# The first q and k of an attention kernel loaded by halves of the heads, deeper gates on the loads that follow, and a new order

## The chip, the cores and the metric

The kernel runs on one core of one Trainium2 chip. The metric is the device time of one execution in microseconds (us); lower is better. Engines are named as in the profile: PE is the matrix engine (PEld its weight loads), DVE the vector engine, ACT the scalar engine, POOL GpSimd, SP the engine that issues stores and DMA transposes here.

## The reference, cut to what matters

```python
# q, k, v: (4, 8, 768, 64) fp32; w_theta, w_ch: (512, 512); w_tok_r, w_tok_i: (768, 768)
scores = q @ k^T / 8                               # per batch and head
keep   = (key < 8) | (0 <= query - key < 96)       # 8 global keys, a local window of 96
scores = where(keep, scores - slope[h] * dist, -1e9)
x      = softmax(scores) @ v                       # then heads side by side: (4, 768, 512)
theta  = x @ w_theta
y      = w_tok_r @ (x * cos(theta)) + w_tok_i @ (x * sin(theta))   # mixes tokens
u      = x + y
out    = u + relu(u @ w_ch)                        # (4, 768, 512) fp32
```

## The kernel before

**Tiling.** A batch of 768 tokens is cut into three thirds of 256 tokens, each of two tiles of 128. Batch `b` and third `g` give names such as `t100`: most names in the order end in batch, third, then head pair, tile or half. Because the window is 96 wide, a tile of queries needs its own tile of keys and the one before it, plus the 8 global keys; a copy of the keys with the global ones put in place of its first eight tokens (`kp`, `kg`; `vpa`, `vpb` for the values) serves as "the one before".

**Stages.** For each third: q and k come in with the tokens on the partitions, PE transposes them (`t`, L371), DVE or ACT takes them out of PSUM (`q`, `k`, L380), PE makes the scores (`s`, L451), ACT the exponentials (`x`, L474), PE the values (`v`, L504), DVE divides by the sums (`n`, L515 and L517). In batch 0 the bias is put into PSUM first by a matmul of a scaled identity `sid` with a distance table `dtab` (`bi`, L442); in batches 1 to 3 the exponential is multiplied by a table `etab` on DVE (`m`, L482). After a batch: `xt` turns x (on PE for batches 0 and 1, as a DMA transpose on SP's queue for 2 and 3, L537), `th` is the theta matmul (L549), `cos` and `sin` run on ACT, `z` is the product on DVE, `mx` the token mixing on PE (L592), `u` the sum on DVE, `ut` turns it (on PE for batch 0, by DMA for the others, L624), `ch` is the last matmul (L636), `o` its end on DVE, `st` the store. `tw` and `twc` turn the token weights once.

**Loads.** The first third of batch 0 comes in fp32 by four DMAs of SP's and ACT's queues (`hw00` and `hw01` for q, `hw10` and `hw11` for k) and is cast on DVE (`cast`, L288). Everything else comes as bf16 by 82 DMAs that POOL issues (`load1` to `load82`): 1 to 4 are the second third's q and k, 5 to 8 values, 9 to 12 the last third's q and k, 13 and 14 values, 15 `w_theta`, 16 to 19 the first token weights, 20 to 49 batch 1, `w_ch` (`load28`) and the other token weights (up to `load44`), 50 to 82 batches 2 and 3. From `load20` on each has a gate in front, a 1x1 POOL copy that reads what the load `DEPTH` = 5 places before it has brought (L230). Besides, DMAs of POOL use eight semaphores in turn, so a load waits in any case until the one eight places before it has landed.

**Order.** All engines work in order, and the order is one long list, `ORDER`, written out in the kernel. `name/ENGINE` picks the engine of an operation that could run on two; `name+N` puts N filler matmuls on zeros in front of it on PE (L145, L147). PSUM has four buffers `pa` (biases, scores, theta) and four `pb` (the rest). Eight matmuls on zeros (L341) open the PE's list.

The lines that the change touches most are `first` (L274), `load_qk` and the calls of `batch` (L310 to L334), `trans_qk` (L361) and the `sid` operations (L209).

Of the kernel before, what the change touches and what calls it, by code (L numbers as in the profile page):

```python
# [9 lines left out]
FP = mybir.dt.float32  # L10
# [27 lines left out]
ones6 hw00 hw10 zero rel ones3 tiny hw01 halfpi hw11 warm0 ones5 ones1 ones4 ones2 load1 ones0 ident sid0 far0  # L38
sid2 far1 load2 dtab0 dtab1 dtab2 load3 dtab3 sid4 sid5 etab7 sid1 sid6 sid7 load4 sid3 etab6 bi0000
cast00/DVE bi0001 bi0010 etab3 load5 t0000 cast10/DVE bi0011 q000/DVE etab1 t0010+5 load6 k000/DVE etab2 kg000  # L40
kp000/DVE load7 etab0 cast01/DVE etab5 t0001+27 load8 cast11/DVE etab4 q001/DVE t0011+12 load9 k001/DVE kg001
s000+3 kp001/DVE load10 s001 x0000 x0001 load11 bi0020+3 t0100 x0010 x0011 bi0021 bi0030 load12 q010/DVE t0110
bi0031 s003 k010/DVE load13 s002 x0030 kg010 kp010/DVE x0031 load14 vpa00/DVE x0020 vpb00/DVE x0021 bi0100+6
load15 v003 v000 v001 load16 bi0101 n000 s010 vpa01/DVE load17 bi0110 x0100 bi0111 vpb01/DVE s011 load18 x0101
n003 bi0120 v002 x0110 load19 n001 bi0121 s012 x0111 n002 bi0130 x0120 v010 bi0131 n010 s013 x0121 v011 x0130
v012 n011 t0200 x0131 n012 t0210 q020/ACT bi0200 k020/DVE xt00 bi0201 xc00/ACT bi0210 kp020/DVE bi0211 kg020
v013 vpa02/DVE s020 n013 s021 x0200 vpb02/DVE xt01+6 x0201 bi0220 gate20 x0210 xc01/DVE bi0221+1 load20 v020
x0211 s022 n020 tw00 gate21 x0220 v021 load21 twc00/DVE bi0230 x0221 bi0231 n021 s023 gate22 th000 x0230
load22 x0231 v022 tw10 ts0 gate23 n022 tw11 load23 v023 twc10/DVE th001 n023 gate24 twc11/ACT load24 tw01 xt02
cos000 twc01/DVE gate25 th011 sin000 load25 xc02/DVE cos001 z000 gate26 th010 load26 sin001 th020 z001 cos010  # L50
gate27 load27 sin010 th021 cos011 z010 gate28 t1000 sin011 load28 tw21 cos020 q100/DVE mx000 gate29 sin020
twc21/DVE load29 t1010 cos021 z011 gate30 mx010 sin021 k100/DVE load30 tx1 vpa10/DVE mx001 gate31 kg100 load31
vpb10/DVE z020 mx011 gate32 kp100/DVE load32 z021 tw20 s100 twc20/DVE s101 gate33 mx002 x1000 load33 x1001
x1010 mx012 u00 x1011 gate34 load34 s102 m101 s103 tw30 u01 x1020 gate35 mx020 x1021 m100 load35 x1030 m102
x1031 mx022 gate36 twc30/DVE load36 m103 mx021 gate37 load37 ut00 u02 ut01 uc00/ACT v102 gate38 t1110 uc01/DVE
load38 tw31 k110/DVE ch01 twc31/ACT gate39 kp110/DVE load39 t1100 kg110 o01 v101 v103 q110/DVE gate40 v100
st01 tw41 load40 ch00 n100 twc41/ACT n101 gate41 ut02 load41 tw40 vpa11/DVE uc02/ACT mx030 o00 twc40/ACT
gate42 vpb11/DVE load42 st00 mx032 n102 n103 mx031 gate43 load43 s110 gate44 u03 s111 load44 x1100 t1200 ch02
x1110 gate45 q120/DVE load45 x1101 ut03 x1111 t1210 m110 gate46 uc03/ACT s112 load46 m111 s113 k120/ACT mx040
o02 gate47 x1120 load47 mx041 kp120/DVE st02 x1121 kg120 gate48 x1130 tw51 m112 load48 v110 twc51/ACT tw50  # L60
n110 v111 mx042 gate49 x1131 n111 load49 twc50/ACT vpa12/DVE s120 u04 s121 gate50 x1200 mx050 load50 m113
x1210 vpb12/DVE ut04 x1201 gate51 ch03 uc04/DVE load51 x1211 m120 s122 o03 gate52 s123 x1220 mx051 load52 m121
x1230 st03 v113 x1221 gate53 xt10 n113 load53 x1231 mx052 m122 ts1 gate54 v120 load54 u05 v112 v121 v122 n112
xc10/ACT ut05 gate55 ch04 n120 load55 uc05/DVE th100 vpa20/DVE gate56 m123 load56 ch05 cos100 vpb20/DVE n121
gate57 sin100 v123 load57 xt11 n122 th101 n123 xc11/ACT gate58 load58 o04 xt12 cos101 o05 th110 st04 gate59
sin101 xc12/DVE load59 st05 th111 cos110 z100 gate60 sin110 th121 z101 load60 cos111 z110 th120 sin111 gate61
vpa21/DVE load61 z111 t2100 cos120 t2010 gate62 vpb21/DVE sin120 load62 t2000 q210/DVE cos121 mx110 z120
gate63 sin121 q200/DVE load63 mx111 k200/ACT z121 gate64 t2110 tx2 load64 kg200 mx112 kp200/DVE k210/DVE
gate65 s200 u11 load65 s201 mx100 x2000 kp210/DVE x2001 ut11 kg210 gate66 x2010 mx101 m200 load66 x2011 s202
m201 gate67 s203 t2200 vpa22/DVE load67 x2020 x2021 t2210 vpb22/DVE x2030 q220/DVE v200 gate68 mx102 x2031  # L70
load68 n200 k220/ACT s210 m203 gate69 s211 m202 load69 x2100 mx120 kp220/DVE x2101 u10 gate70 mx122 x2110
load70 m210 x2111 ut10 s212 kg220 gate71 v202 m211 v201 x2120 load71 ch11 n202 x2121 n201 gate72 v203 s213
load72 n203 mx140 x2130 m212 xt20 gate73 x2131 v210 load73 vpa30/DVE s220 n210 v211 x2200 mx121 gate74 n211
x2201 load74 vpb30/DVE s221 m220 s222 gate75 x2210 ch10 load75 u12 x2211 m213 v220 x2220 ut12 mx130 gate76
x2221 m221 load76 s223 n220 v221 gate77 x2230 m222 mx141 load77 x2231 n221 v222 ts2 gate78 v212 m223 mx131
load78 n212 v223 gate79 n222 v213 load79 mx132 n223 n213 gate80 th200 xt22 load80 o11 mx142 vpa31/DVE cos200
gate81 xt21 u13 load81 sin200 ch12 vpb31/DVE u14 gate82 th201 ut13 load82 o12 mx150 o10 cos201 ut14 z200
sin201 mx151 z201 st12 mx152 st11 th221 st10 u15 t3110 ut15 t3010 k310/DVE t3000 k300/DVE t3100 kp310/ACT
th211 q300/DVE q310/ACT kp300/DVE th210 kg300 kg310 vpa32/DVE th220 cos210 vpb32/DVE sin210 t3210 cos211 t3200
z210 ch13 k320/ACT q320/DVE mx200 sin211 kp320/DVE cos220 o13 ch14 sin220 z211 st13 cos221 mx210 z220 sin221  # L80
o14 mx201 tx3 z221 st14 s300 kg320 s301 mx202 x3000 x3010 mx212 x3001 u20 x3011 m300 s302 ut20 s303 m301 ch15
x3020 x3021 x3030 mx211 o15 x3031 s310 m303 st15 s311 u21 x3100 mx220 x3101 m302 ut21 v300 x3110 mx222 m310
x3111 n300 mx221 m311 v301 u22 v303 v302 v310 n302 ch20 ut22 n301 mx230 o20 n303 ch21 st20 n310 xt30 s312 o21
s313 x3120 mx232 x3121 st21 v311 x3130 mx231 n311 x3131 m312 s320 s321 u23 x3200 mx240 x3201 m313 ut23 v312
x3210 ch22 n312 x3211 m320 s322 s323 o22 x3220 mx241 x3230 m321 st22 v313 x3221 mx250 n313 x3231 m322 ts3 v321
xt31 v320 m323 mx252 n320 v322 v323 n321 ch23 n323 th300 n322 o23 xt32 mx242 cos300 sin300 th301 u24 st23 z300
th310 ut24 cos301 sin301 mx251 cos310 z301 th311 sin310 u25 mx300 z310 cos311 ut25 sin311 th320 z311 th321
cos320 sin320 mx301 cos321 z320 ch24 sin321 z321 mx310 o24 mx302 st24 mx312 u30 mx311 ut30 ch25 u31 mx320 ut31
o25 mx322 st25 mx321 ch30 u32 mx330 ut32 o30 mx331 st30 ch31 mx332 o31 mx340 st31 u33 mx341 ut33 mx342 ch32
u34 mx350 ut34 o32 mx352 st32 mx351 ch33 u35 ut35 o33 ch34 uc35/ACT st33 ch35 o34 ch351 o35 st34 o351 st35  # L90
st351
# [4 lines left out]
def kernel(  # L96
# [13 lines left out]
    nc = tc.nc  # L110
# [51 lines left out]
    DEPTH = 5  # L162
# [46 lines left out]
    for h in range(H):  # L209
        add(f"sid{h}", {"DVE": 0.14},  # L210
            lambda h=h: nc.vector.tensor_scalar(sid[:, h], rel[:, 0], 0.0, -slopes[h] / scale,
                                                op0=ALU.is_equal, op1=ALU.mult),
            reads=["rel"], writes=[("sid", h)], prio=-5)
# [60 lines left out]
    def first(i, t):  # L274
        key, st = ("qk", 0, 0), ("stage", i, t)
        eng = ("SP", "ACT")[i]

        def fn():
            a = new(st, "e", [T, H, D], FP)
            (nc.sync, nc.scalar)[i].dma_start(out=a, in_=(q, k)[i][0, :, t * T:(t + 1) * T, :].rearrange("h p d -> p h d"))  # L280

        add(f"hw{i}{t}", {eng: 0.5}, fn, writes=[st], alloc={st: "e"}, prio=-300 + t,
            lat=(0.9, (0.98, 0.7, 1.75, 0.88)[2 * t + i], 1.45), after=["hw00"] if i + t else [])

        def cast():
            if key not in tiles:
                new(key, "qk", [T, 2, 2, DM], BF)
            vector[o.took](out=tiles[key][:, i, t].rearrange("p (h d) -> p h d", d=D), in_=tiles[st])  # L288

        o = add(f"cast{i}{t}", {"DVE": 0.34, "ACT": 0.49}, cast, reads=[st], writes=[key, key + (i, t)],  # L290
                alloc={key: "qk"} if (i, t) == (0, 0) else None, after=["cast00"] if (i, t) != (0, 0) else [])
# [446 lines left out]
```

The softmax here doesn't subtract the row's maximum and nothing guards it: scores larger than these inputs give would overflow.

## Time and profile before

| | us |
|---|---|
| median of 13 runs | 173.7 |
| lowest and highest of them | 172.57, 175.48 |
| the profiled execution's own time | 173.7 |
| its span, first to last instruction | 171.9 |
| PE busy | 162.7 (95%) |
| DVE busy | 133.9 (78%) |
| ACT busy | 105.9 (62%) |
| POOL busy | 84.1 (49%), all of it before 104 us |

The profiled execution agrees with the median, so its 1.8 us outside the span can be taken as fixed. A busy PE is not the same as a PE at its peak: the ends of matmuls are modelled, and fillers count as busy. So the rows by stage are read together with the starts of the matmuls in the timeline. The granted TensorE clock is 1.00 in every row from the start to the last slice.

### The profile page before, as it was taken

The page shows a single profiled execution, that of the slowest core. Times are in us where ns is not written, and L with a number is a line of the kernel's source. Part 1 is how long each engine was busy: PE and PEld are TensorE (multiplying, and loading weights), DVE is VectorE, ACT ScalarE, POOL GpSimd, SP SyncE. Part 2 cuts the span into 40 slices and gives each one's busy share as a digit, 9 for nine tenths or more (in the row PEclk, how much of TensorE's full clock was granted, in tenths as well). Part 3 has the DMA queues.
Part 4 walks back from the last instruction along what each step waited for, and adds up shares of the span by engine and source line. Part 5 has one row for each costly group of instructions (what it writes and reads, how often), then busy time and mean ns, then how long its engine had stood idle before and what let it go on. Part 6 is the DMA issues. An engine that isn't in the chain of part 4 may idle for free.

```text
span 171.9 us, 4153 instructions
## 1 busy us (share of the span) xinstructions
PE 162.7 (95%) x1598; PEld 92.9 (54%) x1623; DVE 133.9 (78%) x315; ACT 105.9 (62%) x187; POOL 84.1 (49%) x150
## 2 busy tenths in 40 slices
PE   7998999999999899999999999899999999999991
PEld 2664776555666456664555545544555644444440
DVE  7948886798898699999998997695987976634442
ACT  3954988996446887899867622799517847300010
POOL 8997249769897699698888870000000000000000
PEclk9999999999999999999999999999999999999999
DMA  5999999999999999999999999912345365134334
GB/s 123 187 154 155 188 175 117 157 175 150 151 163 191 183 113 157 98 197 121 126 138 139 136 139 164 273 65 87 96 107 138 103 81 131 57 91 127 93 92 183
DMA packets 96868, 23.73 MB, mean 138 GB/s; under 512 B 91088, under 2 KB 93904, under 8 KB 96848
## 3 DMA queue, kind: packets, MB, share of 16 engines
q0 software_dynamic: 73504, 12.33, 97.4%
q1 hardware_dynamic: 21264, 10.62, 25.4%
q10 hardware_dynamic: 2080, 0.52, 1.7%
q8 instruction: 12, 0.20, 0.5%
q14 instruction: 8, 0.07, 0.1%
HBM read 25.69 MB, written 6.29 MB: 186 GB/s over the span
## 4 chain that ended last, share of the span: by engine, by line
DMA 41%; PE 38%; POOL 11%; issue 6%; DVE 1%; DVEq 0%; POOLq 0%
PE pb L592 20%; DMA qk<-in_q_dram 15%; PE pb L636 8%; DMA qk<-in_k_dram 6%; DMA w_theta_bf<-in_moe_w_theta_dram 5%; PE pa L549 5%; DMA xT<-x 4%; POOL qk L243 4%; DMA w_nat<-in_moe_w_tok_i_dram 4%; POOL scrap L230 4%; DMA w_ch_bf<-in_moe_w_ch_dram 3%; DMA vn<-in_v_dram 3%; POOL vn L257 3%; PE pa L504 2%; PE pa L451 2%
## 5 line engine op out<-in xcount | busy, mean ns | idle before, releaser
L592 PE MATMUL pb<-zri,w_tokT 128*128 128x512 bf16 x273 | 67.3, 380 | 1.1 <-issue 0.5
L474 ACT ACTIVATE e<-pa 128x512 bf16<-128x512 f32 (+1 forms) x96 | 46.6, 568 | 20.6 <-PE pa L451 19.9
L592 PEld LDWEIGHTS <-w_tokT 128*128 128x128 bf16 x288 | 26.2, 98 | 28.2
L604 DVE TENSOR_TENSOR u<-x,pb 128x512 bf16<-128x512 bf16 x24 | 16.4, 682 | 11.4 <-PE pb L592 11.2
L636 PE MATMUL pb<-w_ch_bf,uT 128*128 128x512 bf16 (+1 forms) x96 | 24.0, 371 | 0.2
L549 PE MATMUL pa<-w_theta_bf,xT 128*128 128x512 bf16 x93 | 22.5, 380 | 0.5 <-DMA xT<-x 0.4
L482 DVE TENSOR_TENSOR e<-e,etab 128x1024 bf16<-128x1024 bf16 (+1 forms) x36 | 22.4, 637 | 0.7 <-ACT e L474 0.5
L558 ACT ACTIVATE cs<-pa,halfpi 128x512 bf16<-128x512 f32 x24 | 16.6, 692 | 9.8 <-PE pa L549 9.6
L257 POOL DMA_DIRECT2D vn<-in_v_dram x24 | 21.5, 899 | 1.6 <-issue 1.4
L243 POOL DMA_DIRECT2D qk<-in_q_dram x22 | 19.5, 884 | 1.6 <-issue 0.8
L570 DVE TENSOR_TENSOR zri<-x,cs 128x1024 bf16<-128x1024 bf16 x24 | 16.1, 683 | 5.3 <-ACT cs L560 5.3
L243 POOL DMA_DIRECT2D qk<-in_k_dram x22 | 19.4, 881 | 0.6 <-issue 0.6
L642 DVE SCALAR_TENSOR_TENSOR o<-pb,u 128x512 f32<-128x512 f32 (+1 forms) x25 | 16.2, 662 | 3.8 <-PE pb L636 3.7
L504 PEld LDWEIGHTS <-e 128*128 128x128 bf16 x352 | 14.4, 98 | 5.2 <-DVE e L482 0.3
L517 DVE TENSOR_TENSOR x<-pa,rec 128x256 bf16<-128x256 f32 x36 | 15.3, 424 | 1.2
L451 PE MATMUL pa<-qT,kk 64*128 64x128 bf16 x352 | 15.4, 218 | 0.4 <-DVE x L517 0.2
L451 PEld LDWEIGHTS <-kk 64*128 64x128 bf16 x352 | 10.0, 94 | 10.1 <-issue 8.0
L620 ACT COPY uT<-pb 128x512 bf16<-128x512 bf16 x4 | 2.4, 595 | 20.9 <-PE pb L616 20.9
L549 PEld LDWEIGHTS <-xT 128*128 128x128 bf16 x96 | 8.9, 98 | 10.5 <-DMA xT<-x 0.5
L560 ACT ACTIVATE cs<-pa 128x512 bf16<-128x512 f32 x24 | 14.4, 601 | 0.0
L371 PE MATMUL pb<-ident,qk 128*128 128x128 bf16 x192 | 13.7, 220 | 0.4 <-DVE qk L288 0.3
L636 PEld LDWEIGHTS <-uT 128*128 128x128 bf16 x100 | 9.0, 98 | 8.4 <-ACT uT L620 0.3
(69 smaller groups left out, 207.3 us busy)
## 6 DMA issues: line engine op xcount, KB each, us to landing
out_dram<-o SPq DMA_DIRECT2D x23, 256.0 KB, 2.4
vn<-in_v_dram POOLq DMA_DIRECT2D x24, 128.0 KB, 5.5
qk<-in_q_dram POOLq DMA_DIRECT2D x22, 128.0 KB, 5.6
qk<-in_k_dram POOLq DMA_DIRECT2D x22, 128.0 KB, 5.5
w_nat<-in_moe_w_tok_r_dram POOLq DMA_DIRECT2D x6, 192.0 KB, 5.9
w_nat<-in_moe_w_tok_i_dram POOLq DMA_DIRECT2D x6, 192.0 KB, 6.4
e<-in_k_dram ACTq DMA_DIRECT2D x2, 256.0 KB, 5.7
e<-in_q_dram SPq DMA_DIRECT2D x2, 256.0 KB, 5.0
```

The lines of the kernel that those rows point to most:

```text
L243: nc.gpsimd.dma_start(out=tiles[key][:, i, t].rearrange("p (h d) -> p h d", d=D), in_=(q, k)[i][b, :, r0:r0 + T, :].rearrange("h p d -> p ...
L257: nc.gpsimd.dma_start(out=v_bufs[i][:, t, :, 0:D], in_=v[b, :, r0:r0 + T, :].rearrange("h p d -> p h d"))
L451: nc.tensor.matmul(p_[hh][:, s], lhsT=tiles["kk", b, kg][R, kt, p, r, :], rhs=tiles["qT", b, g][R, qt, p, :], start=not biased, stop=not b ...
L474: nc.scalar.activation(tiles[ek][:, hh, 0:n], tiles[pb[hh]][:, 0:n], AF.Exp, scale=scale)
L482: nc.vector.tensor_mul(e_[:, :, 0:n], e_[:, :, 0:n], etab[:, 2 * p:2 * p + 2, s0:s0 + n])
L504: nc.tensor.matmul(o, lhsT=l_, rhs=r_, start=(i == 0), stop=(i == len(mms) - 1))
L549: nc.tensor.matmul(p_, lhsT=tiles["xT", b, g][:, p, t, :], rhs=w_theta_bf[:, p, :], start=(p == 0), stop=(p == NP - 1))
L558: nc.scalar.activation(tiles[ck][:, 0], tiles[ps], AF.Sin, bias=halfpi)
L592: nc.tensor.matmul(p_, lhsT=w_tokT[wi][:, 2 * g + t, tt * T:(tt + 1) * T], rhs=tiles["z", b, g][:, t, wi, :], start=(n == 1 and t == 0 and ...
L604: nc.vector.tensor_add(u.rearrange("n (p c) -> n p c", p=NP), tiles["x", b, tt // 2][:, :, tt % 2, :], tiles[ps].rearrange("n (p c) -> n p ...
L636: nc.tensor.matmul(p_, lhsT=tiles["uT", b, tt][:, p, :], rhs=w_ch_bf[:, p, i * w:(i + 1) * w], start=(p == 0), stop=(p == NP - 1))
L642: nc.vector.scalar_tensor_tensor(o_[:, c], in0=tiles["ch", b, tt, i], scalar=0.0, in1=tiles[uk][:, c], op0=ALU.max, op1=ALU.add)
```

## The change

The four first loads no longer split by tokens but by heads: `hw00` brings q of heads 0 to 3 for all 256 tokens, `hw01` that of heads 4 to 7, and likewise for k. Partition p gets the tokens 2p and 2p+1, which lie side by side in memory, so a run is 512 bytes where it was 256, and there are 512 runs per load where there were 1024. The casts put even tokens and odd tokens apart; after PE's transposes the columns of a tile are all even tokens and then all odd ones, and the copies out of PSUM (now L431) put them back in their places by an access pattern: they read PSUM with a step of 128 elements. The scores of head pairs 0 and 1 need only the first half.

The loads of batch 1 are gated eight places back (`DEPTH1`), and so are the other token weights and `w_ch` between them; `DEPTH` for batches 2 and 3 goes from 5 to 6. All of batch 1's loads have a gate, as before.

The eight `sid` operations move from DVE to POOL: seven between `load1` and `load2`, one between `load5` and `load6`.

The order is new throughout. Fillers before: 5, 27 and 12 in front of three of the first four transposes, 3 at `s000`, 3 at `bi0020`, 6 at `bi0100`, 6 at `xt01`, 1 at `bi0221`. After: 8, 13 and 9, then 5 at `bi0020`, 1 at `bi0110`, 5 at `s020`, 6 at `xt01`, 1 at `bi0221`. Nineteen copies change between DVE and ACT, among them `k000` and `q001` (to ACT) and `xc00` (to DVE). `SPLIT0`, `TQ` and `ORD == 3` are switches that stay off.

```diff
-    DEPTH = 5
+    DEPTH = 6
+    DEPTH1 = 8
...
-        add(f"sid{h}", {"DVE": 0.14},
-            lambda h=h: nc.vector.tensor_scalar(sid[:, h], rel[:, 0], 0.0, -slopes[h] / scale,
+        add(f"sid{h}", {"POOL": 0.2},
+            lambda h=h: nc.gpsimd.tensor_scalar(sid[:, h], rel[:, 0], 0.0, -slopes[h] / scale,
...
-            a = new(st, "e", [T, H, D], FP)
-            (nc.sync, nc.scalar)[i].dma_start(out=a, in_=(q, k)[i][0, :, t * T:(t + 1) * T, :].rearrange("h p d -> p h d"))
+            a = new(st, "e", [T, H // 2, 2 * D], FP)
+            (nc.sync, nc.scalar)[i].dma_start(
+                out=a, in_=(q, k)[i][0, H // 2 * t:H // 2 * (t + 1), 0:2 * T, :].rearrange("h (p j) d -> p h (j d)", j=2))
...
-            vector[o.took](out=tiles[key][:, i, t].rearrange("p (h d) -> p h d", d=D), in_=tiles[st])
+            vector[o.took](
+                out=tiles[key][:, i, :, DM // 2 * t:DM // 2 * (t + 1)].rearrange("p j (h d) -> p h j d", d=D),
+                in_=tiles[st].rearrange("p h (j d) -> p h j d", d=D))
...
-    batch(1, 0, 0)
-    load_w_tok(2, DEPTH)
+    batch(1, 0, 0, DEPTH1)
+    load_w_tok(2, DEPTH1)
...
+        halves = (b, g) == (0, 0)
+        pr = slice(2 * u0, 2 * u0 + 2)
...
+            if halves:
+                p_ = new(ps, "pb", [T, 2, 2, T], BF)
+                fill(p_[:, 0, 0])
+                for p in range(2):
+                    for j in range(2):
+                        nc.tensor.transpose(p_[:, p, j],
+                                            tiles[key][:, i, j, (2 * u0 + p) * T:(2 * u0 + p + 1) * T], ident)
+                return
...
+            if halves:
+                vector[o.took](out=d_.rearrange("c t p (n j) -> c t p n j", j=2),
+                               in_=tiles[ps].rearrange("c p j (t n) -> c t p n j", t=2))
+            else:
+                vector[o.took](out=d_, in_=tiles[ps])
...
-            reads=[(x, b, g, t) for x in ("kk", "qT") for t in range(2)] + [("kk", b, g, 0, "r")] + ([("kk", b, g - 1, 1, "r")] if g else []) + (pb if biased else []),
+            reads=([(x, 0, 0, p // 2) for x in ("kk", "qT")] + [("kk", 0, 0, p // 2, "r")] if (b, g) == (0, 0) else
+                   [(x, b, g, t) for x in ("kk", "qT") for t in range(2)] + [("kk", b, g, 0, "r")])
+            + ([("kk", b, g - 1, p // 2 if (b, g) == (0, 1) else 1, "r")] if g else []) + (pb if biased else []),
```

The start of PE's list, up to the first scores of the last third, before and after:

```
before: warm0 bi0000 bi0001 bi0010 t0000 bi0011 t0010+5 t0001+27 t0011+12 s000+3 s001 bi0020+3 t0100 bi0021 bi0030 t0110
        bi0031 s003 s002 bi0100+6 v003 v000 v001 bi0101 s010 bi0110 bi0111 s011 bi0120 v002 bi0121 s012 bi0130 v010
        bi0131 s013 v011 v012 t0200 t0210 bi0200 xt00 bi0201 bi0210 bi0211 v013 s020
after:  warm0 bi0000 bi0001 bi0010 bi0011 t0000 t0010+8 t0001+13 t0011+9 s000 s001 bi0020+5 t0100 bi0021 s002 t0110
        bi0030 bi0031 s003 bi0100 bi0101 bi0110+1 s010 bi0111 v000 v003 s011 bi0120 v002 v001 bi0121 bi0130 s012 bi0131
        v010 s013 v011 bi0200 v012 bi0201 xt00 t0200 bi0210 t0210 v013 bi0211 s020+5
```

## The prediction

> **What bounds the kernel now.** I read the stage table first (busy us of each engine in 4 us), because the page's shares average over a start, a long middle and a tail.
>
> ```profile
> core 0: us, PE busy (x) PEld busy (x) DVE busy (x) ACT busy (x) POOL busy (x), PEclk, DMA share, GB/s
> 4.00:8.00 4.00, 3.69 (x46) 2.66 (x44) 3.80 (x14) 3.82 (x7) 4.00 (x6) 1.00 1.66 198
> 8.00:12.00 4.00, 3.52 (x51) 2.63 (x49) 2.00 (x6) 2.93 (x7) 3.66 (x5) 1.00 2.47 154
> 12.00:16.00 4.00, 3.54 (x50) 2.34 (x49) 3.13 (x6) 1.65 (x5) 3.85 (x6) 1.00 2.43 156
> 16.00:20.00 4.00, 4.00 (x70) 2.20 (x67) 3.53 (x12) 3.25 (x7) 1.51 (x3) 1.00 2.17 169
> 56.00:60.00 4.00, 3.41 (x39) 1.97 (x38) 2.62 (x8) 3.19 (x7) 2.60 (x7) 1.00 2.02 186
> 108.00:112.00 4.00, 3.56 (x33) 2.20 (x32) 2.49 (x8) 3.17 (x5) 0.00 (x0) 1.00 0.86 264
> ```
>
> From 16 us on PE is busy 3.9 us or more in most rows; 56:60 and 108:112 are the widest holes. Busy ends are modelled, so I checked with the chain of waits:
>
> ```profile
> 100.90 7.51 DMA xT<-x
> ...
> 152.23 2.59 PE pb L592 x12
> 154.82 0.86 PE pb L636 x4
> ```
>
> Twelve 512-wide matmuls in 2.59 us are 0.216 us each with no gap. Charging each PE operation such a pitch (0.216 us for 512 columns, 0.055 for a transpose, 0.24 for eight value matmuls) and walking PE's list in time gives no stall above 0.35 us after 16 us but two: 0.9 us before `tw51` at 57 and 0.43 us at 108. The kernel is bound by PE, and the time is the start, plus PE's fixed work, plus holes. So I cost the change at those places. Before 16 us PE is busy partly with fillers.
>
> ```profile
> 10.37 1.64 ACT L474 ACTIVATE e<-pa 128x384 bf16<-128x384 f32 x4 [1.07 <-PE pa L451]
> 10.91 0.65 PE L147 MATMUL pa<-zero 128*128 128x384 bf16 x3 [0.41 <-ACT e L474]
> 11.40 0.59 PEld L371 LDWEIGHTS <-qk 128*128 128x128 bf16 x8
> 12.97 0.69 DVE L380 COPY kk<-pb 128x1024 bf16<-128x1024 bf16 x1
> 23.45 0.39 POOL L230 COPY scrap<-w_theta_bf 1x1 bf16<-1x1 bf16 x1 [3.65 <-DMA w_theta_bf<-in_moe_w_theta_dram]
> ```
>
> Here the three fillers of `bi0020` first wait for a `pa` buffer that ACT frees, and only then run: they delay `t0100` behind them (11.40). In the last line POOL stands 3.65 us at the gate of `load20`, waiting for `load15`.
>
> **The change part by part.**
>
> *First loads.* The four loads land at 4.67, 5.35, 7.26 and 8.11; `cast11` starts at 8.14, right on the last. 4096 packets of 256 bytes become 2048 of 512. The Trainium skill, "DMA: Bandwidth & Descriptors", Specifications, puts line rate at 512 B and more, with smaller runs paying a read-modify-write. In the trace 1 MB of 256-byte packets needs some 6 us (2 to 8 us), about 170 KB/us; the 1536-byte packets of 20 to 25 us reach about 200, written as bf16 from twice as much read. Rule: packets bound, half the 6 us, last landing near 5. If bytes bind: nothing. I take 1 to 2 us, last landing about 6.5. Either way it isn't the end of the wait, as follows.
>
> *First scores.* `k000` goes to ACT behind five `etab` activations (5.12 us for eight, 0.64 each). DVE sheds eight `sid`, so `dtab` is ready about 0.3 us sooner and the first `etab` starts at 3.85 (4.18 before). ACT: 3.85 + 5x0.64 = 7.05; `k000` 0.6 (as the 0.59 us L620 copy) to 7.65; `kp000`, `kg000` on DVE to 8.25; `s000` at 8.3, before at 9.99. The other two of seven `etab` and `q001` (0.6) end at 9.55, and `x0000` starts at 9.6 (10.37 before). The unpermuting copies read with a step: 512 elements[...] are 0.6 us against the 0.40 of L380 before; 0.2 us each, twice on DVE, behind the `etab` queue; if a strided read took twice that on ACT, `x0000` would lose the 0.8 us again.
>
> *What is left of it.* `bi0020` waits for `x0000` (10.0), then five fillers of 0.16 run where three did, `t0100` comes at about 10.9 (11.40). But `bi0021` and `s002` (0.6 us together) now stand between it and `t0110`, so `k010` starts near 12.8 (12.97), and `kp010`, `kg010`, `vpa00`, `vpb00` follow on DVE as before: `v000` near 15.4, where the first values were at 15.24. PE is then about 1.1 us further in its list (`bi0101`, `bi0110`, `bi0111`, `s010`, 3x0.216+0.49). At `s020` the lists meet again. There DVE decides: `n012`, then `xc00` (0.68, moved from ACT into this place), `k020`, `kp020`, `kg020`. By the rows `k020` is near 21.4 (21.27) and `s020` at 22.8 (22.71), with 1.1 us of fillers ahead of it that mostly cover a wait. Against this, fillers summed up to and with `s020` are 1.15 us shorter, and if they stand for real waits all of that is won. Bounds: -0.3 to +1.15 us gained. I take 0.5, nearer to the chain that I can follow.
>
> *`sid` on POOL.* The rows: `sid` on DVE took 0.20 to 0.36 us; POOL's nearest row is IOTA, 0.34 us for 256 columns, so 0.2 to 0.35 for these 128. The skill's "GPSIMD Engine Reference", Engine selection, speaks against the move: elementwise work belongs on VectorE, GpSimd being about twice as slow with two inputs and near line rate with one. By the rows I take 0.3; by twice DVE's upper value it would be about 0.6. Seven delay `load2` to `load4` by 2.1 us (4.2), but those loads sat behind the first loads' packets anyway (`load4` was issued by 4.96 and landed at 11.42; `load20` took 3.1 us from there). New: 4.96 + 2.1 + 3.1 = 10.2 (12.3), and `t0110` wants it near 12. `bi0011` needs the sixth `sid`: 2.34 + 6x0.3 = 4.1 (5.9), and PE wants it near 5. By the rows it costs nothing, since PE's biases and ACT's tables cover it; by the other price about 1 us, and the sum would be 173.0. It turns at about 0.5 each. I go by the rows. Below nothing there is only DVE's relief, counted above.
>
> *Gates.* Gate 20 waits for `load12` (landed 19.84), not for `load15` (23.39): batch 1 starts some 3.5 us sooner. Later, gate 33's 1.4 us wait for `w_ch` goes as well. The load before `tw51`:
>
> ```profile
> PEld L353 <- DMA w_nat<-in_moe_w_tok_i_dram: 1.0, 1, 1.0
> ```
>
> is `load44`, landed at 58.09. It comes earlier, and the 0.9 us hole closes. At POOL's pitch (0.88 plus 0.18 for its gate; 62 loads from 20.3) the loads would be issued by about 85 and landed by about 95, where the last landed at 108.2. The gates' number stays at 63, and they still cost POOL 0.18 each. Buffers don't hold this: the last third of batch 3 takes the buffers of batch 1's, free by 55.
>
> *Transposes of batch 2's x.*
>
> ```profile
> 99.53 4.06 SPq L537 DMA_TRANSPOSE xT<-x  x2
> DMA to landing us min/median/max: 3.1/4.7/7.9
> ```
>
> The three of batch 2 took 7.9, 5.7 and 7.5 us among the loads; those of batch 3, with the loads over, 3.1 to 3.7. The last one is the 7.51 us in the chain, and the 0.43 us hole. The new order leaves less room: PE work between the last value of a third and its `th` is 7.2, 6.9 and 5.7 us (10.4, 9.5 and 7.2 before). If the loads are over by 97, the two later need about 0.7 (division) + 3.7, and fit; the hole goes, 0.3 us gained. SP's queue is not lengthened: 48 entries as before.
>
> *The rest.* Nineteen copies change between DVE and ACT. A 512-wide one is about 0.4 us on DVE and 0.6 on ACT, hidden while PE's list has other work. The tightest is `twc30` (now ACT, 0.80): PE has 1.2 us between `tw30` and `mx030`. It costs up to 0.3 if ACT is late; I count zero on the sum and keep the end. DVE is 78% busy and isn't next unless the holes move.
>
> **Sum.** Start 0.5, `tw51` 0.9, transposes 0.3: 1.7 us off the profiled 173.7, which is also the median: 172.0.
>
> **The rivals.** *The start is won in full* (1.15, with the holes 1.2): 171.3. For it: `s000` comes 1.7 us earlier. Against: DVE's chain to `s020`. *The start gives it all back* (-0.3), and of the two holes one third remains: 173.7 + 0.3 - 0.8 = 173.2, no change to speak of; also where half the copies moved to ACT open small waits of 0.1 to 0.3 at several places. *Slower by the transposes*: six or eight loads in flight keep the DMA engines fuller at 88 to 106 us, and a transpose on SP's queue waits behind more packets. It decides where landing plus 0.7 passes 7.2, 6.9 and 5.7 us, so from about 5 to 6.5 us. With 7.9, 5.7 and 7.5 as before, PE stands 1.4, 0.7 and 1.3 us, in sum up to 2.5 with two of them overlapping; with the start at zero and `tw51` won: 173.7 + 2.5 - 0.9 = 175.3. For it: those are measured landings; against it: the loads ought to be over by then. *The gates do nothing*, since the eight semaphores hold each load at eight anyway: not so, for five is tighter than eight, as the 3.65 us show.
>
> **How the numbers follow.** Half a per cent, 0.87 us, is about what a measurement of this kernel can tell from none. Main case 0.42 (172.0; faster 0.34, same 0.07, slower 0.01); full start 0.12 (all faster); given back 0.20 (same 0.15, faster 0.02, slower 0.03); slower 0.26 (slower 0.22, same 0.04). Faster 0.48, same 0.26, slower 0.26. The range runs from 170.6, below the full start by its bounds, to 174.9, which leaves out the upper half of the slower case and about 0.05 below. The main case alone is 170.9 to 172.9.
>
> **What would show it.** Right: `s000` near 8.3 and `s020` near 22.2 to 22.8; gate 20 without a wait; no wait of L353's successor for `w_nat`; the last POOL load landed before 100; transposes of batch 2 within 5 us. Wrong: a `sid` of over 0.5 us on POOL with `t0100` or `t0110` waiting for DMA; an L431 copy of over 1 us; a wait of the theta matmul for xT of 1 us or more; or many short PE waits for ACT's `twc` and `k` copies.

## The result: 176.76 us, 1.8% slower

The changed kernel took 176.76 us (median of 11 runs, 175.40 to 177.49). The kernel before, run beside it and over more runs, took 173.69 (48 runs, 172.14 to 175.74). The ratio is 1.0183, with a 95% interval of 1.0157 to 1.0208. Executions more than 1.5% above the fastest of their kernel are left out of every ratio here, while medians and ranges are of all executions. The prediction said 172.0, with a range of 170.6 to 174.9. It was wrong in size and in sign.

The profiled execution took 176.43 us and spans 174.7 us, 2.8 more than before, at a granted clock of 1.00. The stage table of the changed kernel, for the same stretches as before and one more (28:32):

```profile
core 0: us, PE busy (x) PEld busy (x) DVE busy (x) ACT busy (x) POOL busy (x), PEclk, DMA share, GB/s
4.00:8.00 4.00, 3.07 (x27) 1.67 (x26) 1.59 (x4) 3.18 (x6) 3.86 (x6) 1.00 1.06 169
8.00:12.00 4.00, 3.29 (x48) 2.41 (x46) 2.70 (x7) 3.94 (x9) 3.87 (x6) 1.00 1.20 77
12.00:16.00 4.00, 3.63 (x44) 1.94 (x44) 2.25 (x4) 2.32 (x5) 4.00 (x5) 1.00 1.89 122
16.00:20.00 4.00, 2.76 (x47) 1.68 (x46) 3.36 (x8) 2.25 (x5) 4.00 (x6) 1.00 2.11 134
28.00:32.00 4.00, 2.98 (x46) 2.09 (x46) 2.30 (x7) 2.62 (x5) 3.00 (x8) 1.00 1.72 181
56.00:60.00 4.00, 3.95 (x50) 2.67 (x49) 3.69 (x8) 3.93 (x9) 3.88 (x8) 1.00 2.05 182
108.00:112.00 4.00, 3.95 (x43) 2.77 (x43) 3.80 (x7) 1.00 (x2) 0.00 (x0) 1.00 0.88 229
```

The row of the kernel before for the added stretch:

```profile
28.00:32.00 4.00, 3.94 (x50) 2.78 (x48) 3.26 (x8) 3.97 (x8) 3.38 (x8) 1.00 1.62 140
```

The two holes that the prediction wanted to close, 56:60 and 108:112, are closed: PE is busy 3.95 us in both, where it was 3.41 and 3.56. The new holes lie where the kernel before had none: 16:20 has 2.76 us of PE (it had 4.00), and 28:32 has 2.98 (it had 3.94). The last column tells why: from 8 to 16 us the DMA engines move 77 and 122 GB/s, where they moved 154 and 156. POOL is as busy as before, but with something else. POOL's timeline (start, duration, operation), first the issue of `load2` in the kernel before, then the changed kernel:

```profile
2.34 0.88 POOL L243 DMA_DIRECT2D qk<-in_k_dram  x1
...
2.38 4.95 POOL L214 TENSOR_SCALAR sid<-rel 128x128 bf16<-128x128 f32 x7
7.39 0.93 POOL L246 DMA_DIRECT2D qk<-in_k_dram  x1
...
11.18 0.65 POOL L214 TENSOR_SCALAR sid<-rel 128x128 bf16<-128x128 f32 x1
```

Between `load1` and `load2` stand seven `sid`, 4.95 us in all. `load2` is issued at 7.39 where it was at 2.34. The loads behind it, up to `load17`, are issued 5.0 to 5.9 us later as well, and `load18` and `load19` about 3 us. The tile's own rows, before and after, give the lowest, median and highest duration of the eight `sid` in ns:

```profile
L211 DVE TENSOR_SCALAR sid<-rel x8: 202/286/618, 1.6 to 5.0; 128x128 bf16<-128x128 f32 x8
L214 POOL TENSOR_SCALAR sid<-rel x8: 635/640/955, 2.4 to 11.2; 128x128 bf16<-128x128 f32 x8
```

Two groups of PE's waits follow from it. The weight loads of PE near 5 to 13 us and near 29 us, with what ended the idle time in front of each:

```profile
5.45 0.10 PEld L485 LDWEIGHTS <-sid 128*128 128x128 bf16 x1 [0.74 <-POOL sid L214]
6.66 0.10 PEld L485 LDWEIGHTS <-sid 128*128 128x128 bf16 x1 [1.12 <-POOL sid L214]
...
12.54 0.23 PEld L420 LDWEIGHTS <-qk 128*128 128x128 bf16 x4 [0.36 <-DMA qk<-in_q_dram]
...
29.21 0.34 PEld L362 LDWEIGHTS <-w_nat 128*128 128x128 bf16 x6 [0.97 <-DMA w_nat<-in_moe_w_tok_r_dram]
```

and from the list of waits (us in total, times, longest):

```profile
POOL scrap L233 <- DMA w_theta_bf<-in_moe_w_theta_dram: 2.4, 1, 2.4
PEld L485 <- POOL sid L214: 2.1, 3, 1.1
...
PE pb L551 <- DVE vp L455: 1.2, 1, 1.2
```

In the first of these two fences, the first two lines are the biases `bi0010` and `bi0011`, which wait for their `sid`; `t0000`, queued behind them, starts at 6.68 (5.60 before). The others wait for data: the second half of `t0100` for the second third's q (`load3`, landed at 12.50), and `tw00` for its token weights, which came with `load16` at 29.18. In the second fence, the wait of `scrap` is POOL's own, at the gate of `load23` for `load15`. The wait for `vp` is the first value matmuls, which stand until DVE has made `vpb00`; DVE itself stood before `vpa00`:

```profile
16.16 0.56 DVE L452 COPY vp<-vn 128x1040 bf16<-128x1040 bf16 x1 [0.60 <-DMA vn<-in_v_dram]
```

`load6` had brought those values at 16.08 (13.09 before). The chain of work that ended last runs through POOL for its first 21 us and then through one transfer:

```profile
3.84 2.77 POOL sid L214 x4
...
21.70 9.33 DMA w_nat<-in_moe_w_tok_r_dram
```

So the profile alone offers two ways in which `sid` on POOL can cost: late loads, and late biases. The experiments keep them apart.

### The profile page after: what moved, and what is told of

The parts are those of the page before. It is cut to its first block, busy times and chain, and to the rows that moved or that the text cites. A ratio compares the mean times of both kernels' runs of the same rounds, so it can differ in the third digit from the quotient of the medians.

```text
span 174.7 us, 4131 instructions
## 1 busy us (share of the span) xinstructions
PE 163.3 (93%) x1583; PEld 92.5 (53%) x1608; DVE 135.6 (78%) x308; ACT 103.8 (59%) x186; POOL 90.1 (52%) x158
## 4 chain that ended last, share of the span: by engine, by line
PE 65%; POOL 12%; DVE 9%; DMA 9%; issue 3%; ACT 0%; DVEq 0%; POOLq 0%; ACTq 0%
PE pb L639 31%; PE pa L596 11%; PE pb L683 9%; DMA w_nat<-in_moe_w_tok_r_dram 5%; PE pb L420 5%; POOL qk L246 4%; PE pa L494 4%; PE pa L551 3%; DMA uT<-u 3%; POOL sid L214 3%; POOL vn L260 3%; DVE e L529 2%; DVE o L689 2%; PE pb L362 2%; DVE x L564 1%
## 5 line engine op out<-in xcount | busy, mean ns | idle before, releaser
L639 PE MATMUL pb<-zri,w_tokT 128*128 128x512 bf16 x275 | 68.4, 380 | 1.0 <-issue 0.5
L521 ACT ACTIVATE e<-pa 128x512 bf16<-128x512 f32 (+1 forms) x96 | 47.1, 563 | 21.5 <-PE pa L494 21.2
L551 PEld LDWEIGHTS <-e 128*128 128x128 bf16 x352 | 15.4, 98 | 9.1 <-issue 1.3
L667 ACT COPY uT<-pb 128x512 bf16<-128x512 bf16 x6 | 3.6, 592 | 23.1 <-PE pb L663 23.1
L420 PE MATMUL pb<-ident,qk 128*128 128x128 bf16 x176 | 12.8, 220 | 0.2 <-DMA qk<-in_q_dram 0.2
```

Source lines behind the costliest of these rows:

```text
L420: nc.tensor.transpose(p_[:, t - u0, p], tiles[key][:, i, t, p * T:(p + 1) * T], ident)
L521: nc.scalar.activation(tiles[ek][:, hh, 0:n], tiles[pb[hh]][:, 0:n], AF.Exp, scale=scale)
L551: nc.tensor.matmul(o, lhsT=l_, rhs=r_, start=(i == 0), stop=(i == len(mms) - 1))
L639: nc.tensor.matmul(p_, lhsT=w_tokT[wi][:, 2 * g + t, tt * T:(tt + 1) * T], rhs=tiles["z", b, g][:, t, wi, :], start=(n == 1 and t == 0 and ...
```

## The experiments

Eleven kernels were run in three sets, each set beside the kernel before. The latter's median was 174.37, 174.67 and 173.91 in the three sets, and 173.69 beside the changed kernel. So kernels of different sets are compared by their ratios to it (95% interval in brackets), and places in time by the profiled executions.

*Theory A*: POOL's elementwise instructions cost time because they stand in front of the loads in POOL's queue. *Theory B*: they cost time because PE's biases wait for them. The rest of the change was also taken apart: the gates, the halves, the order and the fillers.

### `sid` back on DVE

```diff
-            lambda h=h: nc.gpsimd.tensor_scalar(sid[:, h], rel[:, 0], 0.0, -slopes[h] / scale,
+            lambda h=h: nc.vector.tensor_scalar(sid[:, h], rel[:, 0], 0.0, -slopes[h] / scale,
```

The base is the changed kernel; all else stays, the order too.

> The changed kernel with its eight sid operations on DVE again, all else (order, halves, gates, fillers) kept. Theory A (sid takes 0.65 us on POOL where the sum had 0.3, so load2 and all loads behind it go out 5 us later, and the biases hold up the first transpose by 1.1 us): load2 issued at 2.3 instead of 7.4, t0000 at about 5.6 instead of 6.7, s020 near 22.5, v000 near 15.4, time 172.3 to 173.5. Rival C (the halves, the fillers or the new order are slower by themselves): 175.5 or more, with s020 still near 23.5.

Measured: 172.73 us (172.38 to 172.78), ratio 0.9902 [0.9874, 0.9930]. The whole loss is gone, and the rest of the change is a gain of 1.0%. The price of eight instructions is the difference of the ratios, 2.8 points (1.0183 to 0.9902), or some 4.9 us. The two profiled executions, both at a granted clock of 1.00, lie 3.65 us apart (176.43 and 172.78). The traces explain these 3.65 us. Part of the rest may be the clock: five executions of the changed kernel had a mean granted clock of 0.99, where none of this kernel, with `sid` on DVE, was below 0.996. `load2` is issued at 2.34 again, and the stage table has no hole at 16:20 or 28:32:

```profile
16.00:20.00 4.00, 4.00 (x79) 2.68 (x76) 3.69 (x14) 3.38 (x7) 2.28 (x7) 1.00 1.84 184
28.00:32.00 4.00, 4.00 (x41) 2.46 (x38) 2.85 (x7) 3.97 (x7) 4.00 (x10) 1.00 1.74 185
```

This shows that `sid` on POOL is the cause, but not by which way.

### POOL kept busy at the same places, with `sid` on DVE

```diff
+    dummy = const.tile([T, 2, T], BF, name="dummy")
+    for h in range(H):
+        add(f"dum{h}", {"POOL": 0.2},
+            lambda h=h: nc.gpsimd.tensor_scalar(dummy[:, h % 2], rel[:, 0], 0.0, -slopes[h] / scale,
+                                                op0=ALU.is_equal, op1=ALU.mult),
+            reads=["rel"], writes=[("dum", h)], prio=-250 + h)
...
-sid5 sid0 dtab1 sid1 dtab2 sid2 dtab3 sid4 ident sid3 etab3 sid6 load2
+sid5 dum5 sid0 dum0 dtab1 sid1 dum1 dtab2 sid2 dum2 dtab3 sid4 dum4 ident sid3 dum3 etab3 sid6 dum6 load2
```

(and `dum7` at the place of `sid7`). Nobody reads `dummy`. The biases get their `sid` from DVE in time; the loads are as late as in the changed kernel.

> As e1_sid_dve, with sid on DVE, but the eight POOL operations are issued all the same, at the same places in POOL's queue, onto a scratch tile that nobody reads. It keeps the delay of the loads and takes away PE's wait for the biases. Theory A, the loads being what costs: load2 issued near 7.4, v000 near 15.5 to 16, tw00 waiting for its token weights, time 175.3 to 176.5. Theory B (the biases' wait costs, the late loads are covered): 172.5 to 173.5, as e1_sid_dve.

Measured: 176.98 us, ratio 1.0145 [1.0103, 1.0188]; in the same set, `sid` back on DVE is 0.9902. The time is 0.5 us above the expected range, in a set whose kernel before was 0.7 us slower than beside the changed kernel. The late loads alone cost 2.4 points, and the changed kernel lost 2.8; the intervals overlap. So Theory A holds. Two lines of the waits, and the two stages:

```profile
PEld L427 <- DMA qk<-in_q_dram: 1.7, 1, 1.7
PEld L369 <- DMA w_nat<-in_moe_w_tok_r_dram: 1.2, 2, 0.9
...
12.00:16.00 4.00, 2.71 (x30) 1.49 (x31) 1.96 (x5) 1.60 (x4) 3.99 (x5) 1.00 1.88 123
28.00:32.00 4.00, 3.11 (x48) 2.10 (x47) 2.38 (x7) 2.67 (x5) 3.12 (x8) 1.00 1.84 175
```

Here PE has done its biases early (`bi0011` at 5.21), and then stands 1.7 us in the middle of `t0100` for `load3`, which landed at 13.20. In the changed kernel part of that wait was spent at the biases. The traces also decide about Theory B. At the first value matmuls that wait for `vpb00` the two kernels stand level, at 17.65 (changed) and 17.64, and so they do at `t0200` and within 0.1 us at `tw00`: PE's wait for the biases has left nothing behind. The 0.8 us by which the changed kernel ends later arises at 73 and 100 us, far from the biases. Side by side (us from the start of the span; a load by its landing, an operation by its start):

| | before | changed | `sid` on DVE | POOL busy, `sid` on DVE |
|---|---|---|---|---|
| `load2` issued | 2.34 | 7.39 | 2.34 | 7.67 |
| `load4` landed | 11.42 | 13.38 | 10.42 | 13.99 |
| `load6` landed | 13.09 | 16.08 | 12.06 | 15.84 |
| `load12` landed | 19.84 | 21.73 | 18.49 | 21.85 |
| `load16` landed | 24.39 | 29.18 | 22.83 | 29.08 |
| `bi0011` | 5.78 | 6.67 | 5.16 | 5.21 |
| `t0110` | 12.16 | 13.31 | 12.51 | 14.02 |
| `t0200` | 20.14 | 22.15 | 20.18 | 22.14 |
| `tw00` | 25.43 | 29.22 | 26.14 | 29.12 |
| `v323` | 137.12 | 139.84 | 136.19 | 139.06 |
| `st351` | 168.88 | 171.60 | 167.95 | 170.82 |

Against `sid` on DVE the changed kernel is 0.8 us late at `t0110`, 1.9 at the first values, 3.1 at `tw00`, 3.4 at `tw10` (31.08) and 3.65 at the end, where a wait of 0.2 us for a transpose at 100.34 has come on top. The steps up to `tw10` come where PE or DVE waited for a load (`load3`, `load6`, `load16` and `load18`). And their size can be worked out. `load16` landed 6.35 us later; with `sid` on DVE it had landed at 22.83 and was wanted at 26.14, a slack of 3.3; what is left is 3.0, against 3.1 measured. For `load3` it is 2.96 less a slack of 2.2 (9.54 to 11.71), against 0.8 measured; for `load18` it is 6.3 less 2.9 (24.74 to 27.68), against 3.4. So what counts is the largest remainder of lateness less slack, and not the sum of the waits.

### `sid` on POOL in the kernel before

```diff
-        add(f"sid{h}", {"DVE": 0.14},
-            lambda h=h: nc.vector.tensor_scalar(sid[:, h], rel[:, 0], 0.0, -slopes[h] / scale,
+        add(f"sid{h}", {"POOL": 0.2},
+            lambda h=h: nc.gpsimd.tensor_scalar(sid[:, h], rel[:, 0], 0.0, -slopes[h] / scale,
```

> The kernel before with its sid operations on POOL, at their places in its own list, nothing else. Theory A (0.65 us each on POOL): bi0001 waits for sid1 until about 7.3, t0000 near 7.6 instead of 5.6, load5 issued near 9.5 instead of 4.9; 2.5 to 4 us slower than before, 176.3 to 178. Were sid 0.3 us as in the sum: at most 1 us slower. Were it the mixture with the new order that costs: no slower than 174.5.

Measured: 179.72 us, ratio 1.0312 [1.0266, 1.0358]. The direction is as expected; the size is above it. The old order has `sid` at three places in POOL's list, and `sid1` only after `load3`: `bi0001` starts at 7.65, `bi0011` at 10.74 and `s000`, with its fillers, at 16.38 (9.35 before). PE's waits are for `sid`, and there is none for a load of POOL:

```profile
PEld L442 <- POOL sid L211: 5.8, 2, 3.3
PE pa L442 <- POOL sid L211: 4.9, 2, 2.5
```

At `bi0011` PE is 4.95 us later than before, and from 58 us to the end it is 5.5 to 6.3 us late. So in this order it is the way of Theory B that costs, and the late loads hide behind it. Something comes on top that no other profiled execution here shows. The stages, with the granted clock behind the busy times:

```profile
4.00:8.00 4.00, 1.49 (x6) 0.38 (x5) 1.34 (x2) 4.00 (x7) 3.90 (x6) 1.00 1.65 202
8.00:12.00 4.00, 1.64 (x16) 1.30 (x15) 0.42 (x1) 1.03 (x2) 3.86 (x6) 0.62 1.34 86
12.00:16.00 4.00, 4.00 (x42) 4.00 (x41) 2.62 (x6) 0.00 (x0) 4.00 (x6) 0.53 1.61 102
```

PE was mostly idle from 4 to 8 us, and in the next 8 us the clock was granted at 0.62 and 0.53 in the mean. In rows of 2 us it is 0.50 from 10 to 14 us. The 27 fillers took 3.09 us there, and 1.67 before. An estimate from these rows: 5.6 us of busy PE at a clock near 0.56 are some 2.5 us more than at full clock. But one of the five executions had a mean clock of 0.999, where the others had 0.977 to 0.981, and it took 179.72 us all the same. So it is not shown that the clock costs this kernel anything in the end. Without the new order, halves and gates, `sid` on POOL costs 3.1%; with them, 2.8% (1.0183 to 0.9902). It is a loss in either order, by the biases in the old one and by the loads in the new one.

### How far back in the load queue a delay still costs

The eight `dummy` instructions stand together, first between `load8` and `load9`, then between `load19` and `gate20`; `sid` is on DVE.

```diff
-kg001 x0001 load8 bi0020+5
+kg001 x0001 load8 dum0 dum1 dum2 dum3 dum4 dum5 dum6 dum7 bi0020+5
```

> As e2_pool_late (sid on DVE, eight idle POOL operations onto scratch, some 5 us in all), but with all eight between load8 and load9, so that the second third's q and k and the first values come in time. If every load up to the token weights counts, since PE meets each with little to spare: t0200 waits for load12 and tw00 for load16, 175.3 to 177. If only the loads before load9 counted: 172.5 to 173.3, as e1_sid_dve.

```diff
-n012 t0200 xc00/DVE load19 bi0210
+n012 t0200 xc00/DVE load19 dum0 dum1 dum2 dum3 dum4 dum5 dum6 dum7 bi0210
```

> As e10_pool_late_9, with the eight between load19 and the gate of load20. There some six loads are already issued and not landed, so the DMA engines have work while POOL is held: theory, a delay of POOL costs only where the engines run dry, load20 lands at most 2 us later than in e1_sid_dve (27.1) and the time is 172.4 to 173.2. Rival (POOL's issue is the pace of the whole stream, 5 us are 5 us): 175 or more.

Measured: 1.0119 [1.0092, 1.0146] in front of `load9`, and 1.0018 [0.9983, 1.0053] in front of `gate20`, against 0.9902 with none. The first has its profiled run low in its range (174.45 us where the median is 175.84), so its places are surer than its sum: `load11` landed at 21.44 (17.62), the second half of `t0200` waited 1.1 us for it, and `tw00` came at 27.77 (26.14). So most of the price, 2.2 points, is still due when only the loads from the ninth on are late.

```profile
21.48 0.23 PEld L428 LDWEIGHTS <-qk 128*128 128x128 bf16 x4 [1.06 <-DMA qk<-in_q_dram]
```

For the second the expectation (172.4 to 173.2 us) missed. `load20` had slack: it landed at 27.72, and 27.08 without the delay. But each later load was then issued later too: `load28` landed at 39.63 (35.54), `load44` at 53.99 (50.61), and at 50 us DVE stood 1.6 us for the values of batch 1 and PE behind it. So a delay of POOL that PE does not notice where it stands came back some 25 us after it had ended, and cost 1.2 points.

### The gates alone

```diff
-    DEPTH = 5
+    DEPTH = 6
+    DEPTH1 = 8
...
-    batch(1, 0, 0)
-    load_w_tok(2, DEPTH)
+    batch(1, 0, 0, DEPTH1)
+    load_w_tok(2, DEPTH1)
```

(and so for the other loads of batch 1) in the kernel before; order and all else stay.

> The kernel before with the new gates alone (eight deep in batch 1, six in batches 2 and 3), its own order, loads and sid. If the gates are worth what the sum gave: the 3.65 us POOL wait before load20 gone, the 0.9 us hole before tw51 and most of the 0.43 us one at 108 closed, last load landed before 100, 172.4 to 172.9. Rival: PE's order hides it, or fuller DMA engines delay the transposes of batch 2 by 1 us or more: 173.5 to 175.

Measured: 172.31 us (172.02 to 172.75), ratio 0.9881 [0.9849, 0.9912]. This is worth 1.2%, about 2.1 us, and its six executions spread less: the kernel before ran from 173.00 to 176.59 in the same set. The spans of the profiled executions differ by less, 170.7 and 171.9 us. `load44` landed at 50.27 (58.09) and `load82` at 93.71 (108.21). Both holes are closed:

```profile
56.00:60.00 4.00, 4.00 (x48) 2.40 (x50) 3.39 (x10) 3.91 (x7) 4.00 (x8) 1.00 2.09 182
108.00:112.00 4.00, 4.00 (x32) 2.30 (x31) 2.69 (x8) 3.56 (x6) 0.00 (x0) 1.00 0.00 0
```

### The new order with the old gates

The base is the kernel with `sid` back on DVE.

```diff
-    DEPTH = 6
-    DEPTH1 = 8
+    DEPTH = 5
+    DEPTH1 = 5
```

> As e1_sid_dve, with the gates five deep throughout as before. If the gates help: 0.8 to 1.5 us slower than e1_sid_dve, with waits for token weights or x transposes. If they do nothing in the new order: the same within 0.4 us.

Measured: 175.66 us, ratio 1.0065 [1.0033, 1.0097]: 1.6 points behind the same order with the new gates (1.0065 to 0.9902). That is 2.8 us, where 0.8 to 1.5 was expected. With the old gates the new order and the halves together are slower than the kernel before. The last load is now issued at 97.46 and lands at 102.80, and a transpose by DMA on SP's queue is late among the loads. The stage and PE's weight load that waited:

```profile
96.00:100.00 4.00, 2.05 (x24) 0.97 (x22) 3.51 (x9) 3.35 (x6) 2.24 (x4) 1.00 1.90 150
...
99.51 0.55 PEld L683 LDWEIGHTS <-uT 128*128 128x128 bf16 x4 [2.07 <-DMA uT<-u]
```

It is the last matmul of a tile (`ch12`), whose `ut12` was issued at 92.06 and landed at 99.46; with the new gates it took from 91.37 to 95.08. Ahead of this wait PE is 0.7 us later than with the new gates, behind it 2.8. This is the mechanism of the slower rival, at u and not at x.

### Halves with the old order

Two kernels have the first loads by halves and the unpermuting copies, `sid` on DVE and the order of the kernel before; one with gates at 5, one with the new gates.

```diff
-    DEPTH = 6
-    DEPTH1 = 8
+    DEPTH = 5
+    DEPTH1 = 5
```

The edit shown is that of the first, on top of the old `ORDER`; the second leaves the two depths at 6 and 8.

> The change's loads by halves of the heads, casts and unpermuting copies alone: gates five deep, sid on DVE, and the list of the kernel before, in which k000 and q001 stay on DVE. If the halves bring what the sum gave without the new order: the last first load lands near 6.8 instead of 8.1, but s000 stands behind kp000 and the casts on DVE, so 0 to 0.4 us gained: 173.3 to 174.3 beside a before of 173.7 to 174.4. Rival (the stepped copies of 0.69 us cost more than the loads bring): 0.3 to 0.8 us slower than before.

> e6_halves_only with the new gates (eight and six). Gates and halves add up: 1.3 to 2 us faster than e6_halves_only, and within 0.4 us of e3_gates_only (172.3). If the halves cost: 172.6 to 173.1.

Measured: 174.06 us (171.90 to 176.66), 0.9942 [0.9913, 0.9970], and 173.09 (172.12 to 174.13), 0.9910 [0.9885, 0.9935]. The halves by themselves may be worth some 0.6%, in runs that spread over 4.8 us; the medians of all executions (174.06 to 174.67) give only 0.3%. With the new gates nothing of it is left: the intervals of 0.9910 with the halves and 0.9881 without overlap. Both expectations for the second kernel missed. It is 1.0 us faster than the first by the medians and 0.3 points by the ratios, whose intervals overlap, where 1.3 to 2 us were expected; so the gates are not seen to add up here. And 173.09 lies 0.8 us above the gates alone, in the range given for "the halves cost". Beside a slower kernel before (174.67 to 174.37) and with overlapping ratios, that isn't shown either.

### Without the fillers at three places

The base is the kernel with `sid` on DVE: `bi0020+5`, `bi0110+1` and `s020+5` lose their fillers (one of the three edits is shown).

```diff
-kg001 x0001 load8 bi0020+5 x0010
+kg001 x0001 load8 bi0020 x0010
```

> e1_sid_dve without three groups of fillers: the 5 at bi0020, the 1 at bi0110 and the 5 at s020. In e1_sid_dve's trace s020 comes 1.1 us before that of the kernel before, and xt01 right behind it 0.3 us after: the five fillers at s020 run in full. Theory D (fillers here are plain PE work): t0100 near 10.6 instead of 11.4, xt01 1.1 to 1.8 us earlier, 171.0 to 171.9, against 172.7. Rival (they stand for waits that come in their place, or PE runs slower after an idle stretch): 172.4 to 173.

Measured: 172.40 us, 0.9874 [0.9835, 0.9914], so 0.3 points better than with them, which isn't resolved. The time falls in the rival's range. `t0100` comes at 10.57 (11.38), and `v000` at 14.15 (15.18) with a wait of 1.0 us in it, `s020` at 21.36 (21.59, its fillers included) and then 0.7 us of wait. The fillers of `xt01` start 0.6 us earlier, not 1.1 to 1.8. The fillers mostly stand where PE would wait anyway.

### Five tables later on ACT

The same kernel, with `etab4` to `etab7` and `etab2`, which aren't wanted before batch 1, moved behind the exponentials of the first third on ACT's list.

```diff
-t0000 cast10/DVE etab6 load4 q000/DVE
+t0000 cast10/DVE load4 q000/DVE
...
-cast11/DVE etab4 kp000/DVE
+cast11/DVE kp000/DVE
...
-x0031 vpa00/DVE
+x0031 etab4 etab5 vpa00/DVE
```

> e5_no_fillers with five of the eight etab activations moved on ACT's list: two behind x0031, one behind x0131, two among the exponentials of the last third (the tables are first read in batch 1). In e1_sid_dve k000 started at 7.58, right behind the fifth etab, though its transposes were over at 6.55, and x0000 stood behind two more. If ACT's tables bound the first scores: k000 near 6.6, x0000 near 8 instead of 9.8, t0100 near 9.6 to 10, limited by its loads, and 171.0 to 171.9. Rival: the DVE chain to the values and the loads bind next, and the tables only move: 172.0 to 172.6, as e5_no_fillers.

Measured: 171.67 us (171.07 to 172.17), 0.9860 [0.9813, 0.9907], the best median of all and 1.4% below the kernel before. It isn't resolved from the kernel that it starts from (0.9874). The time lies where the tables were expected to bind, but the places do not: `k000` starts at 7.25 (6.6 expected), `x0000` at 9.51 (8 expected, 9.79 before the move), `t0100` at 10.47 (10.57), `s020` at 21.26 (21.36), so 0.1 us is left by then. In this execution DVE's casts are also later (the last two start at 7.19 and 7.95, against 6.80 and 7.13), and ACT waits 0.83 us at `k000` and 0.68 at `q001` for the transposes behind them. So it stays open what the tables would be worth with the casts on time.

## Why the prediction was wrong

**The step that failed is `sid` on POOL**, in its size and, more, in its cover.

- *Size.* The prediction took 0.3 us each "by the rows", from the IOTA of 256 columns at 0.34 us. Measured: 0.64 us each. Its reading of DVE's durations, 0.20 to 0.36 us, left out the longest, 0.62, and twice 0.36 is 0.72 and not 0.6. Still, that other price, from the rule of the Trainium skill ("GPSIMD Engine Reference", Engine selection: elementwise work belongs on VectorE, with GpSimd about twice as slow at two inputs and near line rate at one), was nearer: the ratio of the medians here is 640 to 286 ns, about twice, though the instruction has one input. The nearest row was of another kind of instruction.
- *Cover.* For 0.6 us each the prediction's sum was 173.0, "about 1 us" more. Measured: 3.65 us between the profiled executions, and 2.8 points by the ratios. The cover named was "PE's biases and ACT's tables", and the loads were followed only to `load4`. `load3` and `load4` landed at 12.50 and 13.38 and cost PE 0.8 us. But fifteen more loads without a gate followed in POOL's queue, most of them issued over 5 us later, and the profile of before already showed what slack these had: `load12` landed at 19.84 and the second half of `t0210` wanted it at 20.79; `load16` landed at 24.39 and `tw00` started at 25.43. The wait behind other packets, on which the prediction counted, took up part: `load4` and `load12` were issued 5.3 and 5.6 us later and landed 2.0 and 1.9 later. At `load16` it was used up, with 5.4 and 4.8. That stands against slacks of 0.9 and 1.0 us.

**The steps that held**, and one beside them that did not, seen in the kernel with `sid` on DVE where `sid` hides them in the changed one:

- *First loads.* Predicted: last landing near 6.5, between 5 by the packets and 8.11 by the bytes. Measured: 6.81 in the changed kernel.
- *Unpermuting copies.* Predicted 0.6 us on both engines. Measured 0.69 on DVE and 0.58 on ACT, the two rows of the timeline:

```profile
7.27 0.69 DVE L431 COPY qT<-pb 128x512 bf16<-128x512 bf16 x1 [2.01 <-PE pb L413]
7.93 0.58 ACT L431 COPY kk<-pb 128x512 bf16<-128x512 bf16 x1 [0.82 <-PE pb L413]
```

- *First scores.* `s000` predicted at 8.3; 8.33 with `sid` on DVE, 9.66 in the changed kernel. With `sid` on DVE, `x0000` starts at 9.79 (9.6 predicted) and `v000` at 15.18 (15.4).
- *Start*, which did not hold. Predicted to give 0.5 us, with `t0100` at 10.9. With `sid` on DVE `t0100` comes at 11.38, as before (11.40). The fillers in front of `s020` start at 21.59 and `s020` itself at 22.97 (22.71 before, without fillers), and the fillers of `xt01` come at 23.52 (23.26 before). So the gain at the start is not there when the lists meet again: the rival that gives it back was right on this point.
- *The hole before `tw51`, and the transposes of batch 2.* Predicted 0.9 and 0.3. Both holes closed. The xT transposes of the changed kernel, which answer to 3.1/4.7/7.9:

```profile
DMA to landing us min/median/max: 3.1/3.2/4.1
```

- *Gates.* Gate 20 has no wait, as said. The last load lands at 94.57 with `sid` on DVE (about 95 predicted), at 100.11 in the changed kernel. The gates alone gave 2.1 us by the ratio, where these two holes together were put at 1.2; by the spans of the profiled executions it is 1.2.

By its ratio, 0.9902, the kernel with `sid` on DVE gains 1.7 us, just the sum of the prediction. That is luck: the start, put at 0.5, gave nothing that lasts to `tw00` (26.14, and 25.43 before), and the gates alone give as much as the whole (0.9881, with overlapping intervals).

**The rivals.** *Slower by the transposes* has the sign, but not the place: in the changed kernel the xT transposes are quick, and the wait for a transpose of u (`[0.20 <-DMA uT<-u]` at 100.34) is short. Its mechanism is real, as the new order with gates at 5 shows. The prediction's own list of signs had the right one, "a `sid` of over 0.5 us on POOL with `t0100` or `t0110` waiting for DMA"; but no rival was built on it, and the later loads were not walked along.

**What stays open.** Halves and new order together gain nothing that these runs resolve over the gates alone: 0.9902 against 0.9881. Why the executions with the deeper gates alone spread less was not tried, nor whether the clock has a share in the loss with `sid` on POOL, in the old order or beyond the 3.65 us in the new one.

## What to carry to other kernels

Before an instruction is put on the queue that issues the loads, write down for every load behind it when it lands and when it is wanted: the smallest difference is the slack of the instruction. Here it was 0.9 us in the kernel before (`load12`), against a delay of 5 at the issue and 2 to 5 at the landing. Take the duration of a moved instruction from the same operation on the same engine, and where the trace has none, work the sum through for the dearer end and follow it until the queue has caught up. Undo each edit of a bundle alone: most of what was good here was the gates, in a few lines of the change.

## What was not expected of the hardware

- POOL's tensor_scalar with two operations from fp32 to bf16 takes 0.64 us for 128 columns, nearly twice the 0.34 us of its IOTA of 256 columns (635 to 654 ns for the eight in front of `load9`).
- With `sid` on POOL in the kernel before, the granted clock of TensorE was 0.62 and 0.53 in the two rows of 4 us that follow one in which PE was busy for 1.49 us. The mean over that profiled execution was 0.977; in every other profiled execution here it was 0.996 or more.
- A DMA transpose (`ut12`) took 7.4 us from issue to landing while loads were still coming, and 3.7 us in the kernel whose last load landed at 94.57.
